# Pooled attention and a gelu layer on one Trainium2 core: pools of all heads on 72 rows, batch 1's v let go later, the last row tile stored in two halves

## The chip, the core and the metric

The kernel runs on one core of a Trainium2 chip. A core has five engines with a queue each: TensorE (PE in the profile: matmuls, with PEld for the loads of the stationary operand), VectorE (DVE), ScalarE (ACT), GpSimd (POOL) and SyncE (SP). Transfers are issued from the queues of SP, ACT and POOL and run on 16 DMA engines that all queues share. Engines work side by side and meet at semaphores. The metric is device time of one execution in microseconds (us), the median of several runs.

## The reference

What is computed is an attention with pooled keys and values, and then a layer of two matrix products with a gelu between. The inputs are float32; q, k and v are 8 batches x 8 heads x 576 rows x 64, w_in is 512 x 2048, w_out 2048 x 512.

```python
k_p = k.reshape(B, H, Sp, pool, D).mean(axis=3)      # pool = 8, Sp = 72
v_p = v.reshape(B, H, Sp, pool, D).mean(axis=3)
scores = scale * np.matmul(q, k_p.transpose(0, 1, 3, 2))
attn = softmax(scores)                               # over the 72 pools
x = (attn @ v_p).transpose(0, 2, 1, 3).reshape(B * S, H * D)      # 4608 x 512
h = x @ w_in
g = 0.5 * h * (1.0 + np.tanh(c * (h + 0.044715 * h * h * h)))
out = g @ w_out
```

(`attn` is written out with the maximum and the sum in the reference.)

## The kernel before, in words

**Groups and batches.** The second part runs over 9 groups `g` of 512 rows of x. A group has two stages: p1 (`p1_mm`, L335: 16 column blocks `fo` of 128 hidden units, 4 matmuls of 512 columns each, then `gelu`, L341) and p2 (`p2_mm`, L344: four row tiles of 128 rows, 16 matmuls each, then `store`, L353 and L359). The attention of batch 0 stands ahead of all groups; that of batch `nb = g + 1` is worked into group `g`: its sums and transposes go beside p1 (the lists `side` and `plan`, by `fo`), its scores, exponentials, products and normalization between the matmuls of p2 (the list `todo`, by the number `m` of the matmul of p2 that they stand before). The order of every queue is the order in which the code is written; a semaphore wait holds up everything behind it on that engine's queue.

**Attention.** k's rows come in with eight rows of a pool beside each other (`load_k`), `k_steps` halves them three times on DVE (L138), `trans_k` turns them on TensorE (L173) and copies them into `kTs` (L183 to L194). `qk` (L238) makes scores with pools on the partitions and 288 columns of q; `expo` (L246) takes the exponential; `av` (L260) multiplies with `vps`, whose second half holds eights, so that the same matmul gives the sum of the exponentials; `norm` and `mult` (L267 to L278) divide, into `xT`. Batch 0 has its own forms (`den0`, `inverse0`, `av0`, `mult0`) with `vz` and `ones`.

**The order of pools on the partitions.** 72 pools are 64 and 8. Of heads 0 to 3 the pools are in order on 72 partitions. Of heads 4 to 7 the last 8 pools are on partitions 0 to 7 and the first 64 on partitions 64 to 127; the rest is zero (`pool_rows` gives 72 or 128). So v's first 64 rows of both halves, which `load_v` puts on partitions 0 to 63 and 64 to 127, are added without a change of partition (`v_steps`), and the last 8 rows, which come in beside k's tail in `load_k`, are moved by two DMAs on SP's queue (`v_moves`, L151).

**The loads at the start.** SP and ACT load k and v of batch 0. POOL's queue issues in this order: q of batch 0, w_in, k of batch 1, q of batch 1, the four quarters of w_out, then q of batch 2 (`load_next`). v of batch 1 is loaded from SP's queue; a memset of one column of its tile on DVE (L421), placed between `mult0(0, 0, 4)` and `den0(1, 2, 6)`, holds it back until then:

```python
    nc.vector.memset(vts[1][:, 0, 0:1], 0.0)
    load_v(1, [nc.sync])
```

In group 0 the plan is: `kk` (the sums of batch 1's k, and `v_moves`) beside `fo` 0; the transposes of batch 1's q (L203) and k beside `fo` 12 to 15; `vv` (the sums of batch 1's v, into `vps`) beside `fo` 15. In p2 of group 0 the first `av` of batch 1 stands before matmul 14.

**The end.** In the last group no attention is left. p1 runs in the order that all groups have (blocks 0 to 3 first, interleaved). Of p2's last row tile, columns 0 to 383 and then 384 to 511 are made, copied and stored; a stored tile is four DMAs of 32 rows, for these two parts on SP and ACT in turn.

Of the kernel before, what the change touches and what calls it, by code (L numbers as in the profile page):

```python
# [8 lines left out]
F32 = mybir.dt.float32  # L9
# [9 lines left out]
def kernel(  # L19
# [12 lines left out]
    N = B * S  # L32
# [34 lines left out]
    def load_k(b, engs):  # L67
        rows = k[b].rearrange("h (j l) d -> (h j) (l d)", l=8)
        main = rows[0:128 * KR].rearrange("(p r) c -> p r c", r=KR)
        n = KR // len(engs)  # L70
        for i, eng in enumerate(engs):
            eng.dma_start(out=kts[b % 2][:, i * n:(i + 1) * n], in_=main[:, i * n:(i + 1) * n])
        engs[0].dma_start(out=kts[b % 2][64:128, KR], in_=rows[128 * KR:])
        rows = v[b].rearrange("h (j l) d -> j h (l d)", l=8)
        for i in range(2):
            engs[-1].dma_start(out=kts[b % 2][32 * i:32 * i + 32, KR], in_=rows[64:, 4 * i:4 * i + 4])  # L76

# [39 lines left out]

    kTs = [[consts.tile([128, H, 128], BF16, name=f"kT{i}{e}") for e in range(2)] for i in range(2)]
    kps = [consts.tile([128, KR + 2, D], BF16, name=f"kp{i}") for i in range(2)]

    vps = [consts.tile([128, H, 2, D], BF16, name=f"vp{i}") for i in range(2)]

    vz = consts.tile([128, H, 2, D], BF16, name="vz")
    ones = consts.tile([128, 2, 3, D], BF16, name="ones")
    idle = consts.tile([128, 512], BF16, name="idle")
# [4 lines left out]
    nc.vector.memset(ones, 0.0)  # L130
    for half, j0, j1 in ((0, 0, 128), (1, 0, 8), (1, 64, 128)):
        nc.vector.memset(ones[j0:j1, half, 1], 8.0)

# [14 lines left out]
    def v_moves(b):  # L148

        for i in range(2):  # L150
            nc.sync.dma_start(out=vps[b % 2][64 - 64 * i:72 - 64 * i, 4 * i:4 * i + 4, 0],  # L151
                              in_=kps[b % 2][32 * i:32 * i + 32, KR])

    def v_steps(b):
        t = vts[b % 2]
        w = (vps[b % 2] if b else vz)[:, :, 0]

        def main():
            for i in range(2):
                p = slice(64 * i, 64 * i + 64)  # L160
                add(w[p, 4 * i:4 * i + 4], t[p, :, 0:64], t[p, :, 64:128])

        return [lambda: add(t[:, :, 0:256], t[:, :, 0:256], t[:, :, 256:512]),
                lambda: add(t[:, :, 0:128], t[:, :, 0:128], t[:, :, 128:256]), main]
# [10 lines left out]
    def trans_k_copy(b, e, bank, lower=True, upper=True):  # L175


        tp = half_bank(bank)[0:D, 0:(KR + 1) * 128].rearrange("p (r c) -> p r c", c=128)
        o = kTs[b % 2][e][e * 64:(e + 1) * 64]
        copy = nc.vector.tensor_copy  # L180

        def heads(h0, h1, c0, j0, j1):
            copy(out=o[:, h0:h1, c0:c0 + (j1 - j0) * KR].rearrange("p h (j r) -> p h j r", r=KR),  # L183
                 in_=tp[:, 0:KR, h0 * KH:h1 * KH].rearrange("p r (h j) -> p h j r", j=KH)[:, :, j0:j1])

        if lower:
            heads(0, 4, 0, 0, KH)
        if upper:
            heads(4, H - 1, 64, 0, 16)
            heads(4, H - 1, 0, 16, KH)  # L190
            copy(out=o[:, H - 1, 64:72].rearrange("p (j r) -> p j r", r=KR),
                 in_=tp[:, 0:KR, (H - 1) * KH:128].rearrange("p r j -> p j r"))
            copy(out=o[:, H - 1, 72:128], in_=tp[:, KR, 64:120])
            copy(out=o[:, H - 1, 0:8], in_=tp[:, KR, 120:128])  # L194

# [34 lines left out]

    def pool_rows(pr):
        return Sp if pr < PR // 2 else 128

    def qk(b, c, pr, bank):
        for e in range(2):
            h = 2 * pr + e
            n = pool_rows(pr)
            nc.tensor.matmul(out=PS[:n, bank + e, :CH].rearrange("j (t p) -> j t p", p=32),  # L238
                             lhsT=kTs[b % 2][c][:, h, :n],
                             rhs=qTs[b][:, h // 4, :, h % 4 * 32:h % 4 * 32 + 32],  # L240
                             start=True, stop=True)

    def expo(b, c, pr, bank):
        n = pool_rows(pr)
        e = ep.tile([128, 2, CH], BF16, name="e", bufs=8)
        nc.scalar.activation(out=e[:n], in_=PS[:n, bank:bank + 2, :CH], func=ACT.Exp, scale=1.0 / 64.0)  # L246
        es[b, c, pr] = e
# [6 lines left out]
    def av(b, c, pr, bank):  # L254


        e = es.pop((b, c, pr))
        n = pool_rows(pr)
        for x in range(2):
            nc.tensor.matmul(out=PS[:, bank + x, :CH], lhsT=window(vps[b % 2][:n], 2 * pr + x),  # L260
                             rhs=e[:n, x, :], start=True, stop=True)

# [19 lines left out]
    def den0(c, pr, bank):  # L282
        for x in range(2):
            e = es[0, c, pr + x]
            n = pool_rows(pr)
            for y in range(2):
                one = ones[:n, pr // 2].rearrange("j a d -> j (a d)")[:, 64 - 64 * y:192 - 64 * y]
                nc.tensor.matmul(out=PS[:, bank + x, :CH], lhsT=one, rhs=e[:n, y, :],
                                 start=(y == 0), stop=(y == 1))
# [8 lines left out]
    def av0(c, pr, bank):  # L298
        for x in range(2):
            e = es.pop((0, c, pr + x))  # L300
            n = pool_rows(pr)
            for y in range(2):
                nc.tensor.matmul(out=PS[:, bank + x, :CH], lhsT=window(vz[:n], 2 * (pr + x) + y),
                                 rhs=e[:n, y, :], start=(y == 0), stop=(y == 1))

# [25 lines left out]

    def p1_mm(g, fo, ko, c0=0, c1=GROUP):
        r0 = g * GROUP
        q, j = divmod(fo % 8, 4)
        nc.tensor.matmul(out=PS[:, h_bank(g, fo), c0:c1], lhsT=w_in_b[fo // 8][:, ko, q * 512 + j:(q + 1) * 512:4],  # L335
                         rhs=xT[:, ko, r0 + c0:r0 + c1], start=(ko == 0), stop=(ko == KO - 1))

# [8 lines left out]

    osbs = {}

    def store(g, r, bank, c0=0, c1=DM):
        if (g, r) not in osbs:  # L350
            osbs[g, r] = opool.tile([128, DM], F32, name="osb")
        osb = osbs[g, r]
        nc.vector.tensor_copy(out=osb[:, c0:c1], in_=PS[:, bank, c0:c1])  # L353

        for n in range(4):
            b, col = divmod(g * GROUP + r * 128 + n * 32, S)
            rows = out[b * S:(b + 1) * S].rearrange("(p t e) d -> e t p d", t=TP, e=2)
            eng = nc.scalar if c1 - c0 < DM and n % 2 else nc.sync
            eng.dma_start(out=rows[col // CH, col % CH // 32, :, c0:c1], in_=osb[n * 32:(n + 1) * 32, c0:c1])  # L359

# [29 lines left out]
    for h in range(H):  # L390
        i = h // 4
        nc.tensor.matmul(out=PS[64 - 64 * i:72 - 64 * i, 7, h * D:(h + 1) * D],
                         lhsT=identb[0:64, 32 * i + h % 4:32 * i + 32:4], rhs=kps[0][0:64, KR],
                         start=True, stop=True)
    scores(1, 1, 0)
    den0(0, 0, 2)
    inverse0(0, 0, 2)
    for i in range(2):
        p = slice(64 - 64 * i, 72 - 64 * i)
        nc.vector.tensor_copy(out=vz[p, 4 * i:4 * i + 4, 0],  # L400
                              in_=PS[p, 7, 256 * i:256 * i + 256].rearrange("p (h d) -> p h d", d=D))
    trans_q(0, *QG[2], 5, nc.vector)
# [16 lines left out]
    mult0(0, 0, 4)  # L419

    nc.vector.memset(vts[1][:, 0, 0:1], 0.0)  # L421
    load_v(1, [nc.sync])
    den0(1, 2, 6)
# [12 lines left out]
    for w in vps:  # L436
        nc.vector.memset(w, 8.0)
        nc.vector.memset(w[0:64, H // 2:], 0.0)
        nc.vector.memset(w[0:8, H // 2:], 8.0)

# [4 lines left out]
    for g in range(NG):  # L445
# [16 lines left out]
        if nb is not None:  # L462
# [4 lines left out]
            if g:  # L467
                plan = {2: kk[:1], 3: kk[1:], 7: vv[:1], 8: vv[1:], 9: tk}
            else:
                tq = [lambda a=a, i=i: trans_q(nb, *a, (5, 6, 7, 5)[i], nc.vector) for i, a in enumerate(QG)]  # L470
                plan = {0: kk, 12: tq[:1], 13: tq[1:2] + tk, 14: tq[2:3], 15: tq[3:] + vv}
            for fo, what in plan.items():
# [6 lines left out]
        else:  # L479
# [4 lines left out]
            first += [(fo, 3) for fo in rest + [late]]  # L484
        for fo, ko in first:
            p1_mm(g, fo, ko)
        for fo in range(FO):
            if fo >= 4:
                for ko in range(KO):
                    p1_mm(g, fo, ko)  # L490
# [38 lines left out]
        for m in sorted(todo):  # L529
            for f, a in todo[m]:  # L530
                f(*a)
    for c0, c1, bank in ((0, 384, o_bank(g, 3)), (384, DM, 4)):
        for fo in range(FO):
            p2_mm(g, 3, fo, bank, c0, c1)
        store(g, 3, bank, c0, c1)

# [29 lines left out]
```

The softmax here doesn't subtract the row's maximum and nothing guards it: scores larger than these inputs give would overflow.

## Time and profile before

The median of three runs is 307.33 us (307.14 to 310.01). The profiled execution took 307.9 us; its span, from the first to the last instruction, is 306.1.

| what | us |
|---|---|
| PEld busy | 157.6 |
| p2 matmuls L344 busy, mean of one | 133.9, 0.373 |
| p1 matmuls L335 busy, mean of one | 126.6, 0.379 |
| gelu L341 busy, mean of one | 81.2, 0.603 |
| first matmul of p1 of group 0 | 20.94 |
| first matmul of p2 of group 0 | 37.61 |
| last group: p1 starts, p2 starts | 274.28, 288.09 |
| last copy of the store starts, takes | 302.15, 0.29 |

A group of instructions has its line, engine, operation, tiles as out<-in, shapes and count, then the busy time and the mean in ns of one, then the idle time of the engine just before them and what ended it. In the chain and the timeline the columns are start, length, and what. Matmuls are pipelined: the mean duration of one is longer than the time from one to the next. A line of the DMA view has a queue, its packets, MB and their share of the time of 16 engines. In a table of stretches, each engine's busy time is followed by its number of instructions; the column PEclk is the granted clock of TensorE, and the last two are the DMA engines' busy share and GB/s.

### The profile page before, as it was taken

How to read it: one execution, taken by the hardware profiler on the slowest of the kernel's cores; microseconds unless marked ns; L12 is line 12 of the kernel's file. 1: busy time of each engine (PE TensorE's matmuls, PEld its weight loads, DVE VectorE, ACT ScalarE, POOL GpSimd, SP SyncE). 2: the span in 40 equal slices, each digit the busy share in tenths (PEclk: the TensorE clock that was granted, in tenths of full speed). 3: DMA queues.
4: the chain of work that ended last, by engine and by line, in shares of the span. 5: the costliest groups of instructions: out<-in, count | busy, mean ns of one | idle time of the engine just before them, and what ended most of it. 6: DMA issues, size and time to landing. Idle time of an engine off the chain costs nothing.

```text
span 306.1 us, 4354 instructions
## 1 busy us (share of the span) xinstructions
PE 296.8 (97%) x1528; PEld 157.6 (51%) x1557; DVE 150.5 (49%) x336; ACT 219.0 (72%) x402; POOL 35.0 (11%) x67
## 2 busy tenths in 40 slices
PE   8999899999999999999999999999999999999994
PEld 3555455555555555555555555555555555445543
DVE  5885757572577057805682559245932630120012
ACT  1687489867987798779977898789868986206500
POOL 7102002305003200320014000400000000000000
PEclk9999999999999999999999999999999999999999
DMA  7999987977955962696159827672101210121022
GB/s 221 266 254 264 227 171 139 310 168 184 257 138 113 278 154 53 118 279 154 35 112 250 181 61 103 203 153 71 35 1 36 59 44 0 36 70 35 2 68 69
DMA packets 30806, 41.12 MB, mean 134 GB/s; under 512 B 18176, under 2 KB 18432, under 8 KB 29888
## 3 DMA queue, kind: packets, MB, share of 16 engines
q0 software_dynamic: 7568, 24.38, 33.7%
q1 hardware_dynamic: 22528, 15.14, 21.1%
q10 hardware_dynamic: 688, 1.31, 1.3%
q8 instruction: 12, 0.20, 0.3%
q14 instruction: 10, 0.08, 0.1%
HBM read 36.70 MB, written 9.44 MB: 151 GB/s over the span
## 4 chain that ended last, share of the span: by engine, by line
PE 87%; DMA 11%; issue 1%; ACT 0%; DVE 0%; POOLq 0%
PE PS L344 40%; PE PS L335 37%; DMA qb<-in_q_dram 11%; PE PS L238 5%; PE PS L260 4%; PE PS L173 1%; PE PS L203 0%; ACT e L246 0%; ACT ld L268 0%; ACT ld L267 0%; DVE osb L353 0%; POOLq L550 0%
## 5 line engine op out<-in xcount | busy, mean ns | idle before, releaser
L344 PE MATMUL PS<-w_out_b,gT 128*128 128x512 bf16 (+2 forms) x577 | 133.9, 373 | 0.7
L335 PE MATMUL PS<-xT,w_in_b 128*128 128x512 bf16 x563 | 126.6, 379 | 0.7
L341 ACT ACTIVATE gT<-PS 128x512 bf16<-128x512 f32 x144 | 81.2, 603 | 48.1 <-PE PS L335 48.0
L335 PEld LDWEIGHTS <-w_in_b 128*128 128x128 bf16 x576 | 64.7, 113 | 57.2
L344 PEld LDWEIGHTS <-gT 128*128 128x128 bf16 x592 | 57.0, 97 | 55.7 <-issue 0.4
L353 DVE COPY osb<-PS 128x512 f32<-128x512 f32 (+2 forms) x37 | 25.1, 677 | 98.2 <-PE PS L344 78.6
L278 DVE TENSOR_TENSOR xT<-PS,rc 64x288 bf16<-64x288 f32 x112 | 50.9, 455 | 31.7 <-ACT rc L270 27.5
L246 ACT ACTIVATE e<-PS 72x576 bf16<-72x576 f32 (+1 forms) x64 | 41.0, 647 | 8.8 <-PE PS L238 7.9
L238 PE MATMUL PS<-qT,kT 128*72 128x288 bf16 (+1 forms) x128 | 25.8, 286 | 0.9 <-ACT qT L213 0.6
L270 ACT ACTIVATE rc<-ld 128x288 f32<-128x288 f32 x56 | 24.8, 444 | 1.8
L313 ACT ACT_TABLE_LOAD x17 | 21.8, 1283 | 4.3 <-issue 4.1
L267 ACT ACTIVATE ld<-PS 64x288 f32<-64x288 f32 x56 | 22.8, 408 | 1.3
L268 ACT ACTIVATE ld<-PS 64x288 f32<-64x288 f32 x56 | 22.5, 402 | 1.4
L260 PE MATMUL PS<-e,vp 72*128 72x288 bf16 (+1 forms) x112 | 23.1, 286 | 0.0
L138 DVE TENSOR_TENSOR kt<-kt 128x1280 f32<-128x1280 f32 (+5 forms) x18 | 18.9, 1048 | 7.6 <-DMA kt<-in_v_dram 4.6
L238 PEld LDWEIGHTS <-kT 128*72 128x72 bf16 (+1 forms) x128 | 13.2, 105 | 15.1 <-DVE qT L215 1.2
L453 POOL COPY gate<-qT 1x2 bf16<-1x2 bf16 x6 | 1.0, 174 | 138.5 <-DMA qT<-qb 138.5
L138 DVE TENSOR_TENSOR vt<-vt 128x1024 f32<-128x1024 f32 (+1 forms) x16 | 15.3, 956 | 1.7 <-DMA vt<-in_v_dram 1.4
L183 DVE COPY kT<-PS 64x288 bf16<-64x288 bf16 (+2 forms) x48 | 13.0, 318 | 6.2 <-PE PS L173 6.0
L260 PEld LDWEIGHTS <-vp 72*128 72x128 bf16 (+1 forms) x112 | 11.0, 98 | 3.8
L365 PE MATMUL PS<-idle 128*128 128x512 bf16 x32 | 10.4, 468 | 1.6 <-DVE idle L126 1.2
L76 POOL DMA_DIRECT2D kt<-in_v_dram x14 | 8.0, 586 | 0.1
(48 smaller groups left out, 88.8 us busy)
## 6 DMA issues: line engine op xcount, KB each, us to landing
out_dram<-osb SPq DMA_DIRECT2D x140, 64.0 KB
kt<-in_k_dram POOLq DMA_DIRECT2D x7, 1024.0 KB, 6.0
vt<-in_v_dram POOLq DMA_DIRECT2D x12, 512.0 KB, 8.7
qb<-in_q_dram POOLq DMA_DIRECT2D x7, 576.0 KB, 11.8
w_in_b<-in_moe_w_in_dram POOLq DMA_DIRECT2D x2, 1024.0 KB, 16.8
w_out_b<-in_moe_w_out_dram POOLq DMA_DIRECT2D x4, 512.0 KB, 19.3
vt<-in_v_dram SPq DMA_DIRECT2D x3, 512.0 KB
kt<-in_k_dram POOLq DMA_DIRECT2D x7, 128.0 KB, 6.0
```

What stands on the lines that cost most here:

```text
L138: nc.vector.tensor_tensor(out=o, in0=a, in1=b, op=ALU.add)
L238: nc.tensor.matmul(out=PS[:n, bank + e, :CH].rearrange("j (t p) -> j t p", p=32), lhsT=kTs[b % 2][c][:, h, :n], rhs=qTs[b][:, h // 4, :, h ...
L246: nc.scalar.activation(out=e[:n], in_=PS[:n, bank:bank + 2, :CH], func=ACT.Exp, scale=1.0 / 64.0)
L260: nc.tensor.matmul(out=PS[:, bank + x, :CH], lhsT=window(vps[b % 2][:n], 2 * pr + x), rhs=e[:n, x, :], start=True, stop=True)
L267: nc.scalar.activation(out=ld[0:64], in_=PS[64:128, bank, :CH], func=ACT.Ln)
L268: nc.scalar.activation(out=ld[64:128], in_=PS[0:64, bank + 1, :CH], func=ACT.Ln)
L270: nc.scalar.activation(out=rc, in_=ld, func=ACT.Exp, scale=-1.0)
L278: nc.vector.tensor_tensor(out=xT[rows, pr, col:col + CH], in0=PS[rows, bank + x, :CH], in1=rc[rows], op=ALU.mult)
L335: nc.tensor.matmul(out=PS[:, h_bank(g, fo), c0:c1], lhsT=w_in_b[fo // 8][:, ko, q * 512 + j:(q + 1) * 512:4], rhs=xT[:, ko, r0 + c0:r0 + c ...
L341: nc.scalar.activation(out=gTs[g][:, fo, :], in_=PS[:, h_bank(g, fo), :], func=ACT.Gelu_apprx_tanh)
L344: nc.tensor.matmul(out=PS[:, bank, c0:c1], lhsT=gTs[g][:, fo, r * 128:(r + 1) * 128], rhs=w_out_b[:, fo, c0:c1], start=(fo == 0), stop=(fo ...
L353: nc.vector.tensor_copy(out=osb[:, c0:c1], in_=PS[:, bank, c0:c1])
```

## The change

Four things change together.

The pools of all heads stand in order on 72 partitions: `kTs` (in its columns), `vps`, `vz` and `ones` (in their partitions) shrink to 72, `pool_rows` goes, `trans_k_copy` copies the upper heads with three instructions where there were five, `v_steps` adds v's upper half from partitions 64 to 127 onto partitions 0 to 63, and the last 8 rows of v go by one DMA where there were two, in `load_k` and in `v_moves`.

v of batch 1 is let go in group 0, after the first of the three sums of batch 1's k: the memset and `load_v(1, ...)` become the second entry of `kk`.

In the last group p1 takes the blocks one by one from `fo` 0 on, each in two pieces: columns 0 to 383 as they are, and columns 384 to 511 in another order (`turned`), in which the 128 rows of the last row tile stand with the four 32-row blocks innermost.

The last row tile is made and stored in two halves of 256 columns, each with one copy and one DMA of 128 rows, the first on ACT's queue, the second on SP's.

```diff
-        for i in range(2):
-            engs[-1].dma_start(out=kts[b % 2][32 * i:32 * i + 32, KR], in_=rows[64:, 4 * i:4 * i + 4])
+        engs[-1].dma_start(out=kts[b % 2][0:64, KR], in_=rows[64:])
...
-        for i in range(2):
-            nc.sync.dma_start(out=vps[b % 2][64 - 64 * i:72 - 64 * i, 4 * i:4 * i + 4, 0],
-                              in_=kps[b % 2][32 * i:32 * i + 32, KR])
+        nc.sync.dma_start(out=vps[b % 2][64:Sp, :, 0], in_=kps[b % 2][0:64, KR])
...
-                add(w[p, 4 * i:4 * i + 4], t[p, :, 0:64], t[p, :, 64:128])
+                add(w[0:64, 4 * i:4 * i + 4], t[p, :, 0:64], t[p, :, 64:128])
...
         if lower:
-            heads(0, 4, 0, 0, KH)
+            heads(0, 4, Sp, 0, 4 * KH)
         if upper:
-            heads(4, H - 1, 64, 0, 16)
-            heads(4, H - 1, 0, 16, KH)
-            copy(out=o[:, H - 1, 64:72].rearrange("p (j r) -> p j r", r=KR),
-                 in_=tp[:, 0:KR, (H - 1) * KH:128].rearrange("p r j -> p j r"))
-            copy(out=o[:, H - 1, 72:128], in_=tp[:, KR, 64:120])
-            copy(out=o[:, H - 1, 0:8], in_=tp[:, KR, 120:128])
+            heads(4, H - 1, Sp, 4 * KH, 7 * KH)
+            heads(H - 1, H, 8, 7 * KH, 128)
+            nc.vector.tensor_copy(out=o[:, H - 1, 8:Sp], in_=tp[:, KR, 64:128])
...
-    def p1_mm(g, fo, ko, c0=0, c1=GROUP):
+    def p1_mm(g, fo, ko, c0=0, c1=GROUP, turned=False):
...
+        w = w_in_b[fo // 8][:, ko, q * 512 + j:(q + 1) * 512:4]
+        out, x = PS[:, h_bank(g, fo), c0:c1], xT[:, ko, r0 + c0:r0 + c1]
+        if turned:
+            out, x = out.rearrange("f (p t) -> f p t", p=32), x.rearrange("k (t p) -> k p t", p=32)
+        nc.tensor.matmul(out=out, lhsT=w, rhs=x, start=(ko == 0), stop=(ko == KO - 1))
...
-    for i in range(2):
-        p = slice(64 - 64 * i, 72 - 64 * i)
-        nc.vector.tensor_copy(out=vz[p, 4 * i:4 * i + 4, 0],
-                              in_=PS[p, 7, 256 * i:256 * i + 256].rearrange("p (h d) -> p h d", d=D))
+    nc.vector.tensor_copy(out=vz[64:Sp, :, 0], in_=PS[64:Sp, 7].rearrange("p (h d) -> p h d", d=D))
...
-    nc.vector.memset(vts[1][:, 0, 0:1], 0.0)
-    load_v(1, [nc.sync])
...
+                kk.insert(1, lambda: (nc.vector.memset(vts[1][:, 0, 0:1], 0.0), load_v(1, [nc.sync])))
                 plan = {0: kk, 12: tq[:1], 13: tq[1:2] + tk, 14: tq[2:3], 15: tq[3:] + vv}
...
-        for fo, ko in first:
+        for fo, ko in first if g + 1 < NG else ():
             p1_mm(g, fo, ko)
         for fo in range(FO):
-            if fo >= 4:
+            if g + 1 == NG:
+                for c0, c1, turned in ((0, 384, False), (384, GROUP, True)):
+                    for ko in range(KO):
+                        p1_mm(g, fo, ko, c0, c1, turned)
+            elif fo >= 4:
...
-    for c0, c1, bank in ((0, 384, o_bank(g, 3)), (384, DM, 4)):
+    for c0, bank in ((0, o_bank(g, 3)), (256, 4)):
+        c1 = c0 + 256
         for fo in range(FO):
             p2_mm(g, 3, fo, bank, c0, c1)
-        store(g, 3, bank, c0, c1)
+        osb = opool.tile([128, 256], F32, name="osb")
+        nc.vector.tensor_copy(out=osb, in_=PS[:, bank, c0:c1])
+        b, col = divmod(N - 128, S)
+        t = col % CH // 32
+        rows = out[b * S:(b + 1) * S].rearrange("(p t e) d -> e p t d", t=TP, e=2)
+        (nc.sync if c0 else nc.scalar).dma_start(out=rows[col // CH, :, t:t + 4, c0:c1], in_=osb)
```

## The prediction

> **What bounds the kernel now.** I read the page first, then the chain of waits in order of time, the waits by what was waited for, and the DMA traffic in stretches of 1 us.
>
> ```profile
> span 306.1 us, 4354 instructions
> PE 296.8 (97%) x1528; PEld 157.6 (51%) x1557; DVE 150.5 (49%) x336; ACT 219.0 (72%) x402; POOL 35.0 (11%) x67
> PE 87%; DMA 11%; issue 1%; ACT 0%; DVE 0%; POOLq 0%
> PE PS L203 <- DMA qb<-in_q_dram: 1.4, 1, 1.4
> 8.79 24.89 DMA qb<-in_q_dram
> 33.73 0.45 PE PS L203 x5
> 41.29 0.25 PE PS L260 x2
> ```
>
> TensorE (PE) is busy 97% and is 87% of the chain that ended last. The rest is one transfer: batch 1's q, issued at 8.79 us, lands at 33.68, and TensorE stands 1.41 us for it. From 33.73 to the end TensorE hardly rests. So a thing costs time only if it makes TensorE stand or work longer, or lengthens the last store; removing work from the other engines is worth nothing.
>
> The second look is at who shares the DMA engines. The DMA view for 30 to 31 us (two lines) and for 35 to 36 us (one line), each with packets, MB and share of the 16 engines:
>
> ```profile
> q0 software_dynamic: 62, 0.14, 73.4%
> q1 hardware_dynamic: 62, 0.13, 37.0%
> ...
> q0 software_dynamic: 55, 0.22, 107.6%
> ```
>
> q0 is POOL's queue, in order w_in, k1, q1, four quarters of w_out, q2; q1 is SP's, and what it carries here is v1 (two loads, 512 packets of 2 KB). With both loaded, 62 packets of one go with 62 of the other: a turn each. A v1 packet takes 16 x 0.370 / 62 = 95 ns of an engine; a w_out packet, alone, 16 / 55 = 291 ns. By the 1 us stretches v1 moves from 22.x (4 packets) to 33.x (2 packets).
>
> **The change, part by part.**
>
> *72 rows for all heads.* A matmul's time goes by its columns, not its rows: L238 with 72 and with 128 rows of pools both show 286 ns, L260 285 and 286, L246 647 and 647. DVE loses two small copies per half of a transposed k (0.15 us each), four short memsets, and one of two casts (2 x 0.42 become one of 512 elements, 0.69 by the store's copy). At 11.7 to 14.1 us that is about 0.5 us on the chain from k0 to the first scores, so TensorE's first p1 (20.94) comes up to 0.5 us earlier. v's tail rows go as one DMA instead of two: one POOL issue (0.59 us) less per batch. One add now reads partitions 64-127 and writes 0-63; the copies into the two halves of kT (both 0.45) say that this is free. Worth nothing unless the end follows, see next.
>
> *v1 behind k's first add.* Now v1 goes at 19.0, after a memset on DVE (L421, ends 18.99). Summing its shares by the 1 us stretches, it took 2.55 us of all 16 engines from 22 to 29 and 3.7 by 33.7. Without it there k1's last piece lands at about 27.5 instead of 30.0, and q1 at about 30.0 instead of 33.7: the 1.41 us wait goes. What is late next is v1. The new memset stands behind DVE's first add on k:
>
> ```profile
> 30.00 2.35 DVE L138 TENSOR_TENSOR kt<-kt 128x1280 f32<-128x1280 f32 x2 [2.67 <-DMA kt<-in_v_dram]
> 32.90 1.61 SPq L151 DMA_DIRECT2D vp<-kp  x2
> 38.56 1.94 DVE L138 TENSOR_TENSOR vt<-vt 128x1024 f32<-128x1024 f32 x2
> 40.54 0.87 DVE L138 TENSOR_TENSOR vp<-vt 64x256 bf16<-64x256 f32 x2
> 41.12 0.41 PE L260 MATMUL PS<-e,vp 72*128 72x288 bf16 x2
> ```
>
> The add begins at 27.5 and takes 1.49, so v1 is issued at 29.1. Packets start about 3.7 us after issue on this queue when q0 is full (memset end 18.99 to 22.7; v's move, issued at 32.90, to 36.9): 32.8. By then w_out, behind q1 in q0, has had 2.8 us alone (154 of its 512 packets at 55 a us). The rest shares by turns: 16 / (0.291 + 0.095) = 41 of each per us, 358 in 8.7 us, to 41.5; v1's last 154 go beside q2 at 62 a us, 2.5 us: **v1 is in at 44.0**. Two checks: now it takes 14.9 us from memset to last packet, beside smaller packets, and 29.1 + 14.9 = 44.0; and all these transfers were done when q2 landed (46.3), with the same bytes to move.
>
> Then DVE's two halvings (1.94) and the first add into vp (0.42): vp at 46.4. The next instructions queued on DVE, the products L278, need av's result, so nobody else is hurt. TensorE wants vp after 14 matmuls of p2; av is issued there now at 41.12, and without the q1 wait and 0.5 us of the front it would be at 39.2. It stands instead until 46.4, and everything behind it (TensorE's queue is in order) moves by 46.4 - 41.12 = **+5.3 us**; both early gains are swallowed. Ends: v1 sharing at 62 a us all the way (512 / 62 = 8.3 us, in at 41.1) gives +2.4, v1 last of all at 46.3 gives +7.6. The move of v's tail rows (L151, issued behind v1 on SP) takes 3 us of small packets, in by 46.4 too.
>
> *TensorE's clock after that stand of 7.2 us.* The trace has no stand over 1.41 us after the start, but it has the start:
>
> ```profile
> 1.19 7.27 PE L365 MATMUL PS<-idle 128*128 128x512 bf16 x22 [1.19 <-DVE idle L126]
> 0.00:5.00 5.00, 3.81 (x9) 1.34 (x10) 2.22 (x8) 0.95 (x1) 3.88 (x11) 1.00 0.60 201
> ```
>
> Nine 512-column matmuls in 3.81 us are 423 ns each, at a granted clock of 1.00, against 216 later; the 22 took 7.27 instead of 22 x 0.216 + 0.16 = 4.9. So the first matmuls after rest cost +2.3 us. I take that whole, as the only row after rest; the other end is 0 (a stand of 7 us may be too short).
> "TensorE: Matmul & The Clock Gate" of the Trainium skill, What's actually happening, has the array fall to half clock after an idle window of about 3.4 us; by that the stand is long enough and the 2.3 stay in the sum; without it the sum is 8.25. No row here shows which.
>
> *Last group's p1 in two pieces.* 64 matmuls of 512 columns become 64 of 384 and 64 of 128. Columns alone cost the same: now 64 take 13.98 us with a last drain of 0.16, 216 ns each; the durations at 512, 384 and 128 columns (379, 326, 219) differ by 0.416 ns a column, so 384 take 163 ns, and 128 take 56 (five transposes in 0.28 us in the chain): 219 against 216, +0.2 us, which I leave out. Each piece loads its weights again, hidden: a load's own part, above the 85 ns of an 8-column one, is 28. But the 128-column pieces read xT with a step of 32 elements (64 B) inside, which no moving operand of the trace does. The nearest rows are weights, packed and with a step of four elements:
>
> ```profile
> L344 PEld LDWEIGHTS <-gT 128*128 128x128 bf16 x592 | 57.0, 97 | 55.7 <-issue 0.4
> L335 PEld LDWEIGHTS <-w_in_b 128*128 128x128 bf16 x576 | 64.7, 113 | 57.2
> L392 PEld LDWEIGHTS <-identb 64*8 64x8 bf16 x8 | 0.2, 85 | 0.1
> ```
>
> Above 85 ns, 12 become 28: the step a little more than doubles the reading. If it doubles a moving read, 128 columns take 53 ns more, x 64 = **+3.4 us**, all on TensorE. From 0 (a read that already streams a column per 0.416 ns cannot gain) to 3.4, or more with a longer step; I take 3.4, the only strided row.
> The skill's "SBUF — State Buffer", SBUF: two separate sides, speaks against the change: lines of 16 bytes, full rate only with at least two accesses to a line running. The step of 64 B has one. It gives no price; by it the sum has some loss here, by the packed rows none.
>
> *Last row tile.* Now 384 + 128 columns, four DMAs each; then 256 + 256, one each. TensorE's end stays (512 columns in all). The last copy grows from 0.29 (128) to about 0.42 (between 0.29 and 0.56 for 384), +0.13; the second issue in a row (0.41) goes, and the wait of SP's queue for the 384's issues (0.28 after the copy's end) too. 128 rows of 1 KB are eight packets an engine instead of two of 512 B twice, some +0.1. Sum **-0.45 us** (0 to -0.7).
>
> **Sum:** 5.3 + 2.3 + 3.4 - 0.45 = +10.55. Span 306.1 becomes 316.65, the profiled execution's 307.9 becomes 318.45; that execution stood 0.57 above the median 307.33, so the median becomes **317.9**.
>
> **Rivals.**
> - *The stand, but a strided read that costs nothing* (12 against 28 ns never shows on TensorE's own matmuls): 317.9 - 3.4 = 314.5. Chance 0.22.
> - *The stand, and the clock holds:* 315.6, or 312.2 with a free read. 0.15.
> - *The strided read costs four times the columns* (+10.2 instead of 3.4): 324.7. 0.08.
> - *v1 slips through (not slower).* If v1 is in by 39.2 - 1.94 - 0.42 = 36.8, TensorE does not stand at av. For: 62 a us is seen, and alone v1 needs 3.7 us. Against: it must start at 32.8 and then have all the engines. Then w_out's last quarter, landing at 43.5 now and used by the 25th matmul at 44.2, leaves 0.7 us to gain: 307.33 - 0.7 - 0.45 = 306.2, or 309.6 with the doubled read. 0.15.
> - My forecast: 0.40.
>
> **Range and chances.** 309.5 to 321 holds my case with its bounds (the stand +2.4 to +7.6), the second and third, and the costly half of the fourth; left out are 324.7 and the free half of v1 slipping through. Within 1% (about 3 us, what a measurement of this kernel can tell from no change) ends at 310.4. Slower by more: 0.40 + 0.22 + 0.15 + 0.08 less 0.03 for a short stand = 0.82; same 0.15; faster 0.03, since all possible gains (1.41, 0.5, 0.45) sum to 2.4.
>
> **What would show it.** A long idle of TensorE before the first L260 of batch 1, and DVE's wait for v1 as its releaser, ending near 44; no wait for q1; L238 and L344 slow (twice) for some 4 us after. The last p1 stretch 3.4 us longer than 13.98 with 128-column matmuls at 107 ns instead of 56. End of TensorE to end of span shorter by 0.45. I am wrong if v1's packets start soon after 29.1 or outrun w_out's, or if k1 lands no earlier than now.

## The result, and the profile after

The changed kernel takes 326.65 us (326.46 to 327.20, four runs) where the kernel before, run beside it, takes 307.29: a ratio of 1.061, 95% interval 1.056 to 1.066. Forecast were 317.9, with a range up to 321.0. The direction came out, the size did not.

The page of the kernel after: its span, TensorE's share, the granted clock in 40 slices, and the shares of the chain that ended last.

```profile
span 324.9 us, 4442 instructions
PE 311.8 (96%) x1621; PEld 167.6 (52%) x1621; DVE 145.8 (45%) x297; ACT 219.3 (68%) x402; POOL 31.3 (10%) x60
PEclk9999978999999999999999999999999999999999
PE 84%; DMA 11%; DVE 1%; POOL 1%; issue 0%; SPq 0%; DVEq 0%; POOLq 0%
```

The span is 18.8 us longer, and TensorE's busy time alone has grown by 15.0. DVE and POOL became emptier, which buys nothing. The clock has a dent in slices 6 and 7, some 40 to 57 us from the start. To see where the 18.8 us went, I took from the trace the first matmul of each stage:

| stage | before, us | after, us | difference |
|---|---|---|---|
| front, to the first p1 matmul | 20.94 | 21.55 | +0.61 |
| p1 of group 0 | 16.68 | 15.10 | -1.58 |
| p2 of group 0 | 18.00 | 27.19 | +9.19 |
| all from there to the last p1 | 218.67 | 218.74 | +0.07 |
| p1 of the last group | 13.81 | 24.41 | +10.60 |
| p2 and store of the last group | 18.00 | 17.90 | -0.10 |

Two stages hold everything. The first of them by its wait (engine, tile and line, what it waited for; us in total, times, longest) and by the chain of waits (start, length, what; SPq is SP issuing), kernel after:

```profile
PE PS L244 <- DVE vp L136: 6.8, 1, 6.8
```

```profile
5.62 22.19 DMA kt<-in_v_dram
27.93 1.49 DVE kt L136
29.47 0.60 SPq L80
30.12 14.50 DMA vt<-in_v_dram
44.71 1.24 DVE vt L136
45.97 0.70 DVE vt L136
46.70 0.43 DVE vp L136
47.17 0.66 PE PS L244 x2
```

L244 is `av`, L136 the sums, L80 `load_v`. Read downwards: k1's tail (the last piece of k of batch 1) is in at 27.81, the first sum ends at 29.42, v1 (v of batch 1) is issued at 29.47 and is in at 44.6, DVE halves it, and `av` runs at 47.17. TensorE's last matmul before that ended at 40.32. What followed is in the stretches of the same kernel (stretch, length, PE busy and its matmuls, granted clock, share and GB/s of the DMA engines):

```profile
41.34:44.76 3.42, 0.00 (x0) 1.00 0.61 150
44.76:48.17 3.41, 1.00 (x4) 0.50 0.56 45
48.17:51.59 3.42, 3.42 (x12) 0.50 0.61 137
51.59:55.00 3.41, 3.41 (x19) 1.00 0.27 106
```

From 44.76 us, still within the stand, the clock is at half for two stretches of 3.41 us; 4.42 us of them (47.17 to 51.59) are work, which at half clock loses 2.2. The stage's +9.19 is 6.85 of stand, and the other 2.34 are slow matmuls.

The second stage by groups of instructions, of the kernel after, from 284 to 305 us, with shapes kept apart:

```profile
L321 PE MATMUL PS<-xT,w_in_b 128*128 128x128 bf16 x56 | 14.7, 392 | 0.0
L321 PE MATMUL PS<-xT,w_in_b 128*128 128x384 bf16 x56 | 11.6, 329 | 0.0
```

The 384 packed columns show the 326 to 329 ns of any matmul of that size. The 128 turned ones, which should show about 219, show 392: longer than three times as many packed columns. The granted clock was 1.00 there. `gelu` gives the same from outside; the timeline (start, length, what, idle time before it), first of the kernel after, then of before:

```profile
287.37 0.60 ACT L326 ACTIVATE gT<-PS 128x512 bf16<-128x512 f32 x1 [0.93 <-PE PS L321]
288.89 0.60 ACT L326 ACTIVATE gT<-PS 128x512 bf16<-128x512 f32 x1 [0.93 <-PE PS L321]
```

```profile
281.39 0.60 ACT L341 ACTIVATE gT<-PS 128x512 bf16<-128x512 f32 x1 [0.27 <-PE PS L335]
282.25 0.60 ACT L341 ACTIVATE gT<-PS 128x512 bf16<-128x512 f32 x1 [0.27 <-PE PS L335]
```

A block took 0.864 us and takes 1.526 now: 0.662 more, 165 ns for each of its four turned matmuls.

### The profile page after: what moved, and what is told of

It reads as the page before. It is cut to its first block, busy times and chain, and to the rows that moved or that the text cites. A ratio compares the mean times of both kernels' runs of the same rounds, so it can differ in the third digit from the quotient of the medians.

```text
span 324.9 us, 4442 instructions
## 1 busy us (share of the span) xinstructions
PE 311.8 (96%) x1621; PEld 167.6 (52%) x1621; DVE 145.8 (45%) x297; ACT 219.3 (68%) x402; POOL 31.3 (10%) x60
## 3 DMA queue, kind: packets, MB, share of 16 engines
q10 hardware_dynamic: 632, 1.31, 1.2%
## 4 chain that ended last, share of the span: by engine, by line
PE 84%; DMA 11%; DVE 1%; POOL 1%; issue 0%; SPq 0%; DVEq 0%; POOLq 0%
PE PS L329 38%; PE PS L321 37%; DMA kt<-in_v_dram 7%; PE PS L244 4%; DMA vt<-in_v_dram 4%; PE PS L224 4%; DVE vt L136 1%; PE PS L169 1%; DVE kt L136 0%; POOL w_in_b L104 0%; POOL qb L85 0%; SPq L80 0%; POOL kt L72 0%; POOL kt L73 0%; DVE vp L136 0%
## 5 line engine op out<-in xcount | busy, mean ns | idle before, releaser
L321 PE MATMUL PS<-xT,w_in_b 128*128 128x512 bf16 (+2 forms) x640 | 137.9, 375 | 0.0
L329 PE MATMUL PS<-w_out_b,gT 128*128 128x512 bf16 (+1 forms) x592 | 137.8, 376 | 0.0
L321 PEld LDWEIGHTS <-w_in_b 128*128 128x128 bf16 x640 | 72.1, 114 | 60.4
L334 DVE COPY osb<-PS 128x512 f32<-128x512 f32 x35 | 24.2, 691 | 113.1 <-PE PS L329 112.8
L231 ACT ACTIVATE e<-PS 72x576 bf16<-72x576 f32 x64 | 40.8, 644 | 11.4 <-PE PS L224 10.6
L244 PE MATMUL PS<-e,vp 72*128 72x288 bf16 x112 | 23.6, 291 | 6.9 <-DVE vp L136 6.8
L224 PE MATMUL PS<-qT,kT 128*72 128x288 bf16 x128 | 26.1, 289 | 0.9 <-ACT qT L203 0.6
L224 PEld LDWEIGHTS <-kT 128*72 128x72 bf16 x128 | 14.4, 114 | 15.0 <-issue 1.3
L136 DVE TENSOR_TENSOR kt<-kt 128x1280 f32<-128x1280 f32 (+5 forms) x18 | 18.9, 1047 | 6.3 <-DMA kt<-in_k_dram 3.3
L136 DVE TENSOR_TENSOR vt<-vt 128x1024 f32<-128x1024 f32 (+1 forms) x16 | 15.3, 956 | 7.6 <-DMA vt<-in_v_dram 7.3
L244 PEld LDWEIGHTS <-vp 72*128 72x128 bf16 x112 | 11.1, 100 | 10.5 <-DVE vp L136 7.1
L80 POOL DMA_DIRECT2D vt<-in_v_dram x12 | 7.6, 652 | 0.1
## 6 DMA issues: line engine op xcount, KB each, us to landing
vt<-in_v_dram SPq DMA_DIRECT2D x3, 512.0 KB, 10.6
```

What stands on the lines that cost most here:

```text
L136: nc.vector.tensor_tensor(out=o, in0=a, in1=b, op=ALU.add)
L224: nc.tensor.matmul(out=PS[:Sp, bank + e, :CH].rearrange("j (t p) -> j t p", p=32), lhsT=kTs[b % 2][c][:, h], rhs=qTs[b][:, h // 4, :, h % ...
L231: nc.scalar.activation(out=e, in_=PS[:Sp, bank:bank + 2, :CH], func=ACT.Exp, scale=1.0 / 64.0)
L321: nc.tensor.matmul(out=out, lhsT=w, rhs=x, start=(ko == 0), stop=(ko == KO - 1))
L329: nc.tensor.matmul(out=PS[:, bank, c0:c1], lhsT=gTs[g][:, fo, r * 128:(r + 1) * 128], rhs=w_out_b[:, fo, c0:c1], start=(fo == 0), stop=(fo ...
L334: nc.vector.tensor_copy(out=osb, in_=PS[:, bank])
```

## The experiments

**The last group alone.** The kernel before with the change's last group: p1 in two pieces, the second turned, and the last row tile in two halves.

```diff
+            if g + 1 == NG:
+                for c0, c1, turned in ((0, 384, False), (384, GROUP, True)):
+                    for ko in range(KO):
+                        p1_mm(g, fo, ko, c0, c1, turned)
```

> The kernel before with the change's last group alone: p1 in pieces of 384 and 128 columns, the 128 turned, and the last row tile in two halves with one DMA each. Theory A (the strided read sets the cost, 219 ns for 128 turned columns in the changed kernel's trace against 56 packed): p1 of the last group takes 24.4 us instead of 13.8, the time is 307.3 + 10.6 - 0.1 = 317.8. Theory B (the last group costs the predicted 3.4 and the rest of the loss came earlier): 310.3. The last store, from the last matmul to the end of the span, is 3.9 us against 3.95 before if one DMA a half gains nothing.

Measured: 318.03 us, ratio 1.0336 (1.0307 to 1.0364). The last p1 takes 24.42 us, the stage behind it 17.91; the stages ahead differ from before by 0.5 us at most. So +10.6 belongs to this part by itself, whatever the front does.

**The front alone.** The changed kernel with the last group of before: 72 rows and the late v1.

> The changed kernel with the last group of the kernel before: 72 rows for all heads and batch 1's v let go behind k's first add. Theory A (late v, then a slow clock): TensorE stands until about 47 at the first av of batch 1 and then runs at half clock for some 4 us; 307.3 + 6.05 + 2.25 = 315.6. Theory B (the early part costs only the stand): 313.4.

Measured: 316.85 us, 1.0304 (1.0274 to 1.0333). p2 of group 0 takes 27.46, with a stand from 40.19 to 46.84. The two parts add up: 1.0336 + 0.0304 makes 1.064 beside 1.061 for the whole.

**72 rows alone.** As the last, with v1 issued where it was before.

```diff
+    nc.vector.memset(vts[1][:, 0, 0:1], 0.0)
+    load_v(1, [nc.sync])
...
-                kk.insert(1, lambda: (nc.vector.memset(vts[1][:, 0, 0:1], 0.0), load_v(1, [nc.sync])))
```

> The run before this one with batch 1's v let go where the kernel before has it: 72 rows for all heads alone. As predicted, half a microsecond less on DVE ahead of the first p1 and nothing lost: 306.8. By the changed kernel's trace, where first transpose to first p1 takes 12.55 us as before, it gains nothing: 307.3. If one of the moved partitions or the single DMA of v's tail costs something in each of the 8 batches, it is slower than 308.

Measured: 308.19 us over ten runs, 1.0025 (1.0001 to 1.0048). The stand in group 0 is gone, so the whole of it belongs to v1's place. But p2 of group 1 is 19.19 where it was 17.75. The chain of waits of this kernel in that stretch:

```profile
70.76 1.01 SPq L213
71.82 0.02 SPq L148
71.86 2.05 DMA vp<-kp
73.96 0.42 PE PS L244 x2
```

L213 are the DMA transposes of q3 (q of batch 3) on SP's queue, L148 is `v_moves` of batch 2 behind them. In this execution q3 came in at 69.0 (before: 67.05), the transposes were held back by as much, the move of v's tail rows stood behind them, and TensorE stood 1.25 us for it.

**The same, with the moves first.** From group 1 on, the transposes of q are issued on SP behind `v_moves`.

```diff
         if 0 < g and g + 2 < B:
-            load_next()
+            load_q(g + 2)
...
+                if g + 2 < B:
+                    kk.append(lambda: load_next(False))
```

> The run with 72 rows alone (v let go early), and in every group from 1 on the transposes of the next but one batch's q are issued on SP behind the move of v's tail rows, not ahead of it; the loads that hang on them follow. Theory: in the run with 72 rows the move of batch 2 stood on SP behind transposes that wait for q3 (issued 71.86, landed 73.9) and TensorE stood 1.25 us at the first av; with the move first p2 of group 1 takes 17.76 instead of 19.19 and the time is 306.8. Rival: the 0.6 us of that run come from 72 rows themselves or from chance: 308.2, or 307.5.

Measured: p2 of group 1 is 17.76 again and TensorE has no wait there, so the order on SP's queue was the cause. The time is 307.74 us over ten runs, 1.003 (0.9995 to 1.0065): no difference that can be told, and no gain from the 0.5 us that 72 rows were to save.

**The clock after the stand.** The front alone, with 30 matmuls on zeros put before the first `av` of batch 1; they fill TensorE's stand with work.

```diff
+                    if g == 0 and i == 1:
+                        at(pos[i], spin, 30, 6)
                     at(pos[i], av, *a)
```

> 72 rows and the late v, last group as before, and 30 matmuls on zeros put before the first av of batch 1, 30 x 0.216 = 6.5 us, so that TensorE works through the stand of 6.9 us. If rest is what slows the clock, the matmuls behind the stand run at 216 ns at once and the time is 2 us below the run without them: 313.5. If the clock has nothing to do with rest, it is the same as without them, 315.6. If the 30 outlast the wait for v, it is up to 0.5 us more.

Measured: 314.88 us against 316.85; p2 of group 0 is 25.13 against 27.46, 2.33 less. The stretch from 45 to 50 us (busy time of PE, PEld, DVE, ACT, POOL, then granted clock, DMA share, GB/s) of the front alone, and then of this kernel:

```profile
45.00:50.00 5.00, 2.94 (x8) 1.37 (x10) 3.05 (x6) 1.25 (x3) 0.00 (x0) 0.54 0.90 103
```

```profile
45.00:50.00 5.00, 4.53 (x24) 2.16 (x23) 3.53 (x6) 1.90 (x5) 0.00 (x0) 1.00 0.62 120
```

The clock stays at 1.00 and v1's sums are ready no earlier (47.28 against 46.80). So rest is what slowed the clock, and matmuls that compute nothing bring its share back.

**How the price of a step goes.** The last group alone, with the step of the second piece's columns chosen by block: none for blocks 0 and 1, then 2, 4, 8, 16 and 32 elements of two bytes.

```diff
+            s = (1, 1, 2, 2, 2, 4, 4, 4, 8, 8, 8, 16, 16, 16, 32, 32)[fo]
+            if s > 1:
+                out, x = out.rearrange("f (p t) -> f p t", p=s), x.rearrange("k (t p) -> k p t", p=s)
```

> The run with the last group alone, but the 128-column piece of p1 reads xT with a step that differs by hidden block: 1 (packed) in blocks 0 and 1, 2 in 2 to 4, 4 in 5 to 7, 8 in 8 to 10, 16 in 11 to 13, 32 in 14 and 15 (bf16, so 2 to 64 bytes); the last 128 rows of the output are therefore another sum. From gelu to gelu a block took 0.864 us in one piece and 1.526 with step 32. Theory A, lines of 16 bytes: steps 2 and 4 cost little (0.86 to 0.97), 8, 16 and 32 all 1.53; time 307.5 + 8 x 0.66 = 312.8. Theory B, anything not packed costs four times: all from step 2 on 1.53, 316.7. Theory C, cost by the length of the step: 32 alone 1.53, 16 about 1.2, 8 about 1.0; 310.2. Blocks 0 and 1 give the price of two pieces alone: 0.86.

Measured: 316.46 us in one execution, part of it from a longer wait in group 0 (last section); the last p1 takes 20.28, +6.47 over before. `gelu`s of this kernel in the timeline, one each of the blocks with a step of 2, 4, 8, 16 and 32:

```profile
280.21 0.60 ACT L346 ACTIVATE gT<-PS 128x512 bf16<-128x512 f32 x1 [0.29 <-PE PS L341]
...
283.34 0.60 ACT L346 ACTIVATE gT<-PS 128x512 bf16<-128x512 f32 x1 [0.53 <-PE PS L341]
...
287.61 0.60 ACT L346 ACTIVATE gT<-PS 128x512 bf16<-128x512 f32 x1 [0.98 <-PE PS L341]
...
292.35 0.60 ACT L346 ACTIVATE gT<-PS 128x512 bf16<-128x512 f32 x1 [0.99 <-PE PS L341]
...
296.99 0.60 ACT L346 ACTIVATE gT<-PS 128x512 bf16<-128x512 f32 x1 [0.93 <-PE PS L341]
```

A `gelu` waits for its block, so its distance from the one before (its own 0.60 and the idle time in brackets) is what the block cost TensorE. By the start times:

| step, elements (bytes) | block, us | a 128-column matmul over the packed 56 ns |
|---|---|---|
| 1 (two pieces, packed) | 0.83 | 0 |
| 2 (4) | 0.88 | +4 ns |
| 4 (8) | 1.12 | +64 ns, 2.1 times |
| 8 (16) | 1.57 | +176 ns, 4.1 times |
| 16 (32) | 1.58 | +179 ns, 4.2 times |
| 32 (64) | 1.53 | +166 ns, 4.0 times |

(The third column is a quarter of what the block is above 0.864.) The two pieces cost nothing, the step costs, and its price is flat from 16 bytes on. In "SBUF — State Buffer", SBUF: two separate sides, the Trainium skill has lines of 16 bytes, with the full rate as long as two accesses fall into a line. The flat price from one element a line on fits lines of 16 bytes; a step of 8 bytes has two elements in a line and was not free. So the first theory is the nearest, but wrong at four elements. One thing is left open: as the step grows, the run of columns at that step gets shorter, from 64 at a step of 2 to 4 at a step of 32, and no run here varies the two apart.

**The turn on the way out of TensorE.** As the last group alone, but the columns are read packed and written to PSUM with a step of 16 bytes (four float32).

```diff
-            out, x = out.rearrange("f (p t) -> f p t", p=32), x.rearrange("k (t p) -> k p t", p=32)
+            out, x = out.rearrange("f (p t) -> f t p", p=32), x.rearrange("k (t p) -> k t p", p=32)
```

> The run with the last group alone, but the 128 columns of xT are read packed and the matmul's output is written turned, with a step of four float32 (16 bytes) in PSUM. If only the moving read pays for a step: 307.5 - 0.1 = 307.4, 0.87 us a block. If a strided output pays as much as the strided read: 318.

Measured: 311.36 us, 1.0106 (1.0073 to 1.014); the last p1 takes 17.35, +3.54 over before, 55 ns for each of the 64 matmuls: between the two expectations. By groups, from 284 to 305 us:

```profile
L339 PE MATMUL PS<-xT,w_in_b 128*128 128x128 bf16 x40 | 6.0, 304 | 0.0
```

304 ns where 392 were: a strided write doubles the columns' time where the strided read makes it four times. Read and write have prices of their own.

**The turn in ScalarE.** p1 in one piece as before; `gelu` makes the turn while it works through the last 128 columns. The last row tile is stored as in the change.

```diff
+        if g + 1 == NG:
+            nc.scalar.activation(out=o[:, 0:384], in_=h[:, 0:384], func=ACT.Gelu_apprx_tanh)
+            o = o[:, 384:].rearrange("f (p t) -> f t p", p=32)
+            h = h[:, 384:].rearrange("f (t p) -> f t p", p=32)
+        nc.scalar.activation(out=o, in_=h, func=ACT.Gelu_apprx_tanh)
```

> The kernel before with p1 of the last group block by block and in one piece, and the turn made by ScalarE: gelu of the last group in two instructions, 384 columns packed and 128 written with a step of four bf16; last row tile in two halves as in the change. TensorE's work is that of before, gelu takes about 0.8 us a block against 0.864 between blocks, so nothing waits: 307.4, the single DMAs' -0.1 alone. If the strided write doubles gelu's 128 columns, gelu is the pace of the last p1: 0.95 a block, 309.

Measured: 307.44 us over ten runs, 1.0002 (0.9986 to 1.0019); the last p1 takes 13.81 as before. Two of its `gelu`s in the timeline:

```profile
278.25 0.49 ACT L343 ACTIVATE gT<-PS 128x384 bf16<-128x384 f32 x1
278.63 0.45 ACT L346 ACTIVATE gT<-PS 128x128 bf16<-128x128 f32 x1
```

The turn costs no time here, because ScalarE has just enough to spare: a block's pair of activations takes 0.83 us where one took 0.60, and comes every 0.86 us, TensorE's own pace. And it shows what the turn was to make possible: with it the last stage takes 17.90 us instead of 18.00. Over all profiles that stage takes 17.90 to 18.01 us with single DMAs and 17.91 to 18.02 with four of 32 rows, so a gain of a tenth of a microsecond is not told from scatter.

**v1 on POOL's queue.** 72 rows, the last group as before, and v1 behind q1 (q of batch 1) and ahead of w_out.

```diff
     load_k(1, [nc.gpsimd])
     load_q(1)
+    load_v(1, [nc.gpsimd])
```

> 72 rows, the last group as before, and batch 1's v neither early (behind a memset in the attention of batch 0) nor late (behind k's first add), but on POOL's queue right behind q of batch 1 and ahead of w_out, so that nothing goes beside q and nothing beside v. Theory A (what moves the front is only who shares the DMA engines): q of batch 1 lands at about 30, p1 of group 0 takes 15.1 to 15.5 us instead of 16.7, av of batch 1 does not stand, and the last quarter of w_out, which comes 0 to 1 us later than before, gives some of it back: with the stand of 1.25 us at av of batch 2 that 72 rows alone showed, 306.9 to 308.0. Theory B (v anywhere behind k makes av stand, since its load takes 14.9 us whatever stands beside it): TensorE stands 5 us or more before the first av of batch 1, 314 to 317.

Measured: 309.81 us, 1.007 (1.0046 to 1.0093). The first theory's order of events came out: q1 is in at 30.14 instead of 33.68, and `av` of batch 1 doesn't stand. Its time didn't. w_out's quarters are in at 37.61, 40.07, 42.57 and 44.99, each 1.5 us later than before (36.12, 38.59, 41.09, 43.53), and the waits of TensorE show what is late now:

```profile
PE PS L327 <- DMA w_out_b<-in_moe_w_out_dram: 2.0, 3, 1.3
PE PS L170 <- DVE kp L137: 1.5, 1, 1.5
```

q2 comes 1.45 us later as well (47.78 against 46.32); the loads of k2 are let go behind q2's transposes, 1.4 us later too, and k2's tail lands at 63.92 instead of 59.88, which makes the second wait. Why k2 takes the other 2.7 us longer was not looked for. From q1's landing to v1's there are 5.6 us (35.73 - 30.14), with v1 as 4 KB packets on POOL's queue; on SP's, as 2 KB packets, it took 3.7 us of the engines. Whether the queue or the packet is the reason, no run here separates.

**All that helped by itself.** The last kernel with the moves first and with the turn in ScalarE.

> The same, with q's DMA transposes issued behind v's moves on SP from group 1 on (no stand at av of batch 2), and the last group turned by ScalarE in gelu with single DMAs of 128 rows. Theory A: each part brings what it showed by itself (q's wait about -1.2 in the first p1, 72 rows 0, the end 0 to -0.1): 306.0 to 307.0, the fastest of all, by less than 0.5%. Theory B (w_out's last quarter or v's tail rows take the place of q's wait): 307.0 to 308.5, no better than before.

Measured: 310.49 us, 1.0073 (1.0046 to 1.010). The second theory came out, with more than it had asked: TensorE stands for w_out, once, and then runs at half clock for 3.41 us:

```profile
PE PS L332 <- DMA w_out_b<-in_moe_w_out_dram: 2.2, 1, 2.2
```

A wait at q1 was exchanged for a wait at w_out. No version here beats the kernel before.

## Why the prediction was wrong, and where it was right

**The step that failed** is the strided read: "If it doubles a moving read, 128 columns take 53 ns more, x 64 = +3.4 us". Measured are +165 ns and +10.60 us. The mechanism was right, the term was mis-sized by 7.2 of the 8.2 us that the profiled span is longer than forecast. The row it was taken from (12 against 28 ns of weight loading) had a step of four elements, and at four elements the moving read does a little more than double (+64 ns). The fault was to carry that price over to a step of 32: a step of 8 bytes costs 64 ns, one of 64 bytes 166. The trace of before has no row with a longer step, so the bound "or more with a longer step" should have been the end of the range, and the rival with four times the columns (+10.2, 324.7 us), which came out for this term, had 0.08 and was left outside.

**v1 behind k's first add: right, a little short.** Forecast and measured: k1 in at 27.5 (27.81), v1 issued at 29.1 (29.47), in at 44.0 (44.62), `vp` ready at 46.4 (47.1), a stand of 7.2 (6.85). The wait for q1 went, as said, and was swallowed. `av` came 6.05 us later than before instead of 5.3: 0.3 of it at k1, 0.25 from v1's issue to its landing (15.15 instead of 14.9), and 0.2 in small gaps from one step to the next. v1's first 2 KB packet went at 33.29 (forecast 32.8), and the two queues took turns as put, 41 packets of each in a us; the DMA view of the kernel after for 36 to 37 us:

```profile
q0 software_dynamic: 40, 0.15, 74.6%
q1 hardware_dynamic: 41, 0.08, 24.4%
```

**The slow clock: right, and its size in part by luck.** +2.3 was taken from the start of the kernel; measured are 2.34. The prediction read a granted clock of 1.00 there, but the trace's first record of the clock is at 5.98 us; up to it the matmuls on zeros start 427 ns apart, and so do the p2 matmuls in the stretches at 0.50 of the kernel after. What a stand costs beyond itself goes by the work that falls into the slow stretches: 4.42 us in the kernel after, 5.38 us (46.84 to 52.22) in the front alone, where the stage lost 2.81 (27.46 - 18.00 - 6.65 of stand). The run with matmuls in the stand took back that 2.81, less the 0.48 by which its v1 was ready later: 2.33. "The clock holds" fell.

**72 rows: nothing, and the 0.5 us didn't show either.** From the first transpose of k to the first p1 both kernels take 12.55 us (8.39 to 20.94, 9.00 to 21.55), so what went from DVE was not on that path. In both, the only waits of TensorE in the list of waits for that time are for ScalarE's copy of q (0.6) and for `xT` (0.3), none for a copy of k. The 0.61 us by which the first p1 came later are the matmuls on zeros at the start, 7.88 us in this execution against 7.27; over all profiles the first p1 began between 20.77 and 21.61. The sum was not touched, since the stand swallowed whatever came before it.

**The last store: -0.10 instead of -0.45.** The second issue fell away, as said, but one issue for 128 rows takes longer than one for 32 (0.63 against 0.36 to 0.43). Kernel after, and then before, in the timeline:

```profile
321.07 0.42 DVE L514 COPY osb<-PS 128x256 f32<-128x256 f32 x1 [1.32 <-PE PS L329]
321.52 0.63 SPq L518 DMA_DIRECT2D out_dram<-osb  x1
```

```profile
302.15 0.29 DVE L353 COPY osb<-PS 128x128 f32<-128x128 f32 x1 [0.34 <-PE PS L344]
```

The copy grew by the forecast 0.13. Behind the copy 0.59 us were to go (0.41 and 0.28, less 0.1); from its end to the end of the span there are 3.41 us instead of 3.65, so 0.24 went. The wait for the queue went with 0.25, the issues got 0.29 shorter (0.92 to 0.63) instead of 0.41, and the way from the last issue to the end of the span got 0.30 longer (2.45 to 2.75) instead of 0.1.

The sum as it should have been: 6.05 + 2.34 + 10.60 - 0.10 = 18.9, beside 18.8 measured between the two spans. The medians differ by 19.4: the profiled execution of before lay 0.57 above its median, that of after at its own.

## What to carry to other kernels

Price a new access pattern by a row with the same step in bytes, not by the nearest strided row; where there is none, let the range reach to the highest price that can be named, here four times the packed read. Put a change of order on the engine that has time to spare: the same turn cost 10.6 us in TensorE's read, 3.5 in its write and no time in ScalarE, whose work still fitted into the block's pace. And before a load is moved to clear another's way, ask which load takes the place of the one that is cleared: k, q, v and w_out of the first 46 us had hardly a gap to give, and each order tried here moved the wait to the last in line.

## What the runs showed of the chip that was not expected

**A stand of 2 us was enough for the slow clock, and it is paid in pieces of 3.41 us.** In the runs with the steps, the turn in PSUM and all parts together, q1 or w_out came late enough for one stand of 2.05, 2.51 and 2.23 us, and each was followed by one stretch of 3.41 us at half clock. The stretches of the run with the steps (TensorE stood from 32.23 to 34.27):

```profile
31.94:35.35 3.41, 1.36 (x11) 1.00 1.06 222
35.35:38.76 3.41, 3.41 (x21) 0.50 1.07 213
38.76:42.17 3.41, 3.41 (x22) 1.00 1.07 210
```

Its p1 of group 0 took 18.98 us where before took 16.68. The wait is 0.64 longer; the other 1.66 are about half of a stretch (3.41 / 2 = 1.71). The other two have the same: from 32.37 to 35.78 TensorE was busy 0.95 us of 3.41, from 35.75 to 39.16 1.18 us, and the next 3.41 us were at 0.50. Stands of 1.25 (72 rows alone), 1.31 and 1.51 (v1 on POOL's queue) and 1.41 us (before) left the clock at 1.00; in the first of the two on POOL's queue the stretch had 2.10 busy of 3.41. Nearest to the limit is the front alone, in the stretch where its long stand begins (from 40.19 us) and the one behind it, still at 1.00:

```profile
38.56:41.98 3.42, 1.63 (x9) 1.00 1.07 252
41.98:45.39 3.41, 0.00 (x0) 1.00 0.49 112
```

All this fits a clock that goes by the busy share of a fixed stretch, with a limit between 40% and 48%. "TensorE: Matmul & The Clock Gate", What's actually happening, has windows of about 3.4 us, free-running, and half clock after an idle one; their length is as stated, but the three that brought the slow clock here were not idle, 28 to 40% of each was work.

This also puts a price on a wait that looks small: in these runs it jumps by 1.7 between 1.5 and 2 us (each of the three stands over 2 us lay almost wholly within one stretch; one shared by two was not seen). Three of the ten executions of the kernel with the moves first took 310.6 to 310.9 us, 3 more than the rest, at a mean clock of 0.992 to 0.994 instead of 0.997 to 1.000. One half-speed stretch of 3.41 us makes 0.994 of a span of 306. But executions of the kernel before at 0.991 took 307.92 and 308.14, so the clock alone does not make the 3 us; there is no trace of the three, and that q1's landing was late in them is not shown.

**A strided write to PSUM** of 16 bytes doubled a 128-column matmul (+55 ns), and about half of the weight loads beside it (63 of 128) lengthened too, from 113 to 139 ns. The 55 ns are what TensorE's pace shows of both together.
